# One read back ahead of the loads of v, and one output two products later, in a linear attention and SwiGLU kernel

## The chip, the core and the metric

The kernel runs on one core of a Trainium2 chip. Its engines work side by side: TensorE (PE in the profile: matrix products), VectorE (DVE), ScalarE (ACT), GpSimd (POOL) and SyncE (SP). Here SyncE only issues DMA transfers; GpSimd and ScalarE issue some too. Each engine takes its instructions in the order of its own queue, and a DMA whose buffer is not free yet holds up everything behind it in the queue that issues it. The metric is the device time of one execution in microseconds (us), lower is better.

## The reference

For 4 batches, 8 heads, 768 time steps and a head size of 48 a gated linear recurrence is computed. Its output goes through a SwiGLU block with 384 model dimensions and 1536 hidden ones.

```python
f = 1.0 / (1.0 + np.exp(-f_logit))
for t in range(S):
    state = f[:, :, t, :, None] * state + np.einsum('bhd,bhe->bhde', k[:, :, t], v[:, :, t])
    y[:, :, t] = np.einsum('bhd,bhde->bhe', q[:, :, t], state)
x = y.transpose(0, 2, 1, 3).reshape(B * S, H * D)
g = x @ w_gate
out = (g * (1.0 / (1.0 + np.exp(-g))) * (x @ w_val)) @ w_out
```

All tensors reach the kernel in float32, or as 64-bit words that it converts itself (the weights).

## The kernel before

The 768 steps are cut into 6 chunks of 128. A **unit** is one chunk of one batch, so there are 24; they are numbered u = 4 x chunk + batch from 0. Unit 5 is the second chunk's second unit, units 8 to 11 make up the third chunk. The attention of a unit replaces the recurrence by products within the chunk plus a carried state. Beside the attention of chunk c + 1 runs the SwiGLU block of chunk c: as plain products for the first chunk (gate and val at L940, down product o at L963), and with fewer products but more sums on VectorE from the second chunk on (L1156, L1259, L1322). The first part of the program, up to the block of the first chunk, works with the units 0 to 7; in it the weights are also converted.

`attention(u)` is a generator of 15 steps. What matters here, in order:

- Steps 1 to 4 turn the gates f and the decays (`gates`, `tails`) into the decayed k, `kT` (VectorE, L682 to L649).
- Step 5: `kT` is transposed in blocks (L723, into the room of the raw k) and written to DRAM as `turn` (L726, four transfers). Behind it the next unit's k is loaded into the same room (L498).
- Step 7: q is transposed (L741, into `tails`), and the next unit's q is loaded behind it. Step 8: q times the gates becomes `qT`. In the second chunk the step also loads the part of v that is needed beside A: `load_other_v` (L454, "A<-in_v_dram", two transfers). It writes into a corner of the score buffer `A`, of which there is one, so it waits until the previous unit's y products are done with it.
- Step 9: the scores `sc`. From the third chunk on this is where `load_other_v` is called, and then, for batches 0 to 2, `turn` is read back into `kt` (L784). There is one `kt`, read by the product dS. Step 10 masks the scores into `A`; in the second chunk, and for batch 3, it also holds the read back (L790).
- Step 12, the output: the products of y with the state (L837), the new state's product dS (L819, from `kt` and `v`), and the products of y with A (L848; L873 for the other units). Step 13 copies y out (L855) and sends it into `xT` (L862). From the third chunk on it also loads v of the unit after next (L506), into one of two `v` buffers, which this unit's products just read. Step 14 forms the state (L901).

The transfers of q, k, f, v, `turn` and `kt` are issued by GpSimd for units 5 to 7 (most of them) and by SyncE from unit 8 on.

The order of everything comes from due times written by hand. `EARLY` has one row of 15 times for each unit of the second chunk, one for each step. `times(c)` does the same for the later chunks: the output at time o, step 13 at o + 0.01, step 14 at o + 2.1. `in_turn_of_time` runs down the products of the SwiGLU block, counts 2.57 for each plain product, and calls every step whose time has come. The resulting order is then fixed for PE, VectorE, ScalarE and SyncE; for GpSimd it is fixed only in the later part, so in units 4 to 7 the scheduler may move GpSimd's instructions among each other.

Of the kernel before, what the change touches and what calls it, by code (L numbers as in the profile page):

```python
# [290 lines left out]
def short_path(ctx, tc, ident, least, judge, q, k, v, f_logit, moe_w_gate, moe_w_val, moe_w_out, out):  # L291
# [24 lines left out]
    SQUARES = 2  # L316
# [86 lines left out]
    def by_squares(u):  # L403
        return u >= SQUARES * B - 3
# [24 lines left out]
    def in_halves(u):  # L429

        b, c = units[u]
        return c > 0 and b < B - 1
# [10 lines left out]
    def other_v(A):  # L443

        return A.rearrange("p r a t -> p (r a t)")[:, 12 * CH:].rearrange("p (h e) -> p h e", e=W)

    def load_other_v(A, u):
        b, c = units[u]  # L450
        queue = nc.sync if c >= SQUARES or not by_squares(u) else nc.gpsimd
        for n in range(2):
            since = c * C + (1 - n) * CH
            queue.dma_start(out=other_v(A)[n * CH:(n + 1) * CH, :, 0:D],  # L454
                            in_=v[b, n * HP:(n + 1) * HP, since:since + CH, :].rearrange("h t d -> t h d"))
# [26 lines left out]
    def load(u, what="fkqv"):  # L482
        b, c = units[u]
        rows = slice(c * C, (c + 1) * C)
        inputs = dict(f=f_logit, k=k, q=q, v=v)
        for nm in "fqkv" if c >= SQUARES else "fvkq" if by_squares(u) else "fkqv":
            src = inputs[nm]
            if nm not in what:
                continue
            if nm == "v":  # L490
                dst = v_of(u)
            elif not by_squares(u):
                dst = raw[nm][u % NRAW]
            else:
                since = len(traced)
                for n in range(4):
                    at = Q * (1 - n % 2)
                    (nc.sync if c >= SQUARES else nc.gpsimd).dma_start(  # L498
                        out=rooms[nm][Q * n:Q * (n + 1), at:at + HP * RUN].rearrange("t (a e) -> t a e", a=HP),
                        in_=src[b, n // 2::2, rows, :].rearrange("a (t i) d -> t a (i d)", i=NI))  # L500
                if c < SQUARES:
                    by_pool.extend(ins for ins in traced[since:] if ins.engine == mybir.EngineType.Pool)
                    keep_order(by_pool[-5:])
                continue
            queue = nc.gpsimd if nm == "v" and c < SQUARES and (by_squares(u) or u in (1, 2)) else nc.sync
            queue.dma_start(out=dst[:, :, 0:D], in_=src[b, :, rows, :].rearrange("h t d -> t h d"))  # L506
# [118 lines left out]
    def attention(u):  # L625
        b, c = units[u]
# [13 lines left out]
        halves = in_halves(u)  # L640
# [75 lines left out]
        if turned:  # L716


            if u == SQUARES * B:
                A = att.tile([128, 2, HP, C], FP32, tag="A", name="A")  # L720
# [24 lines left out]
        if halves and c < SQUARES:  # L745
            A = att.tile([128, 2, HP, C], FP32, tag="A", name="A")
# [7 lines left out]
        if u != SQUARES * B and not (halves and c < SQUARES):  # L754
            A = att.tile([128, 2, HP, C], FP32, tag="A", name="A")
        flat = [A.rearrange("p r a t -> p (r a t)")[:, 6 * CH * par:6 * CH * par + 8 * CH] for par in range(2)]
        if halves and c >= SQUARES:
            load_other_v(A, u)
        sc = [score_bank(u) for _ in range(2)]
        for keys in range(2) if halves else ():  # L760
            for a in (0, 2, 1, 3):
# [20 lines left out]
        at_once = turned and c >= SQUARES and b < B - 1  # L782
        if at_once:
            turn_queue.dma_start(out=kt, in_=turn.rearrange("t i a r e -> i t (a r e)"))  # L784
        yield
        if not in_squares:
            nc.scalar.copy(least[:, u, :], whole.rearrange("p a t -> p (a t)"))
# [35 lines left out]
        if halves:  # L823
# [28 lines left out]
            def copy_y():  # L852
                yT = att.tile([128, 2, TB // 2], FP32, tag="x", name="yT")
                for par in range(2):
                    nc.scalar.copy(yT[:, par, :], y[par][:, 0:HP // 2 * C])  # L855
                for h in range(H):
                    a, par = h // 2, h % 2
                    f = h * D
                    while f < (h + 1) * D:
                        n = min((h + 1) * D, (f // 128 + 1) * 128) - f  # L860
                        r = W * (a % 2) + f - h * D
                        (nc.gpsimd if c >= SQUARES else nc.sync).dma_start(out=xT[c][f % 128:f % 128 + n, f // 128, b * C:(b + 1) * C],  # L862
                                                                           in_=yT[r:r + n, a // 2, par * C:(par + 1) * C])
                        f += n
# [26 lines left out]
            dS = new_state()  # L891
        if halves:
            copy_y()
        if c >= SQUARES and u + 2 < len(units):
            load(u + 2, "v")
        yield
        if c == 0:
            nc.scalar.copy(states[b], dS)
        elif c < NCH - 1:
# [133 lines left out]
    def score_bank(u):  # L1033
        b, c = units[u]
        kind = SCORES[c][b][1] if c >= SQUARES else "b"
        if kind == "b":
            return bank("sc")
        return {"o": banks_o, "A": banks_a}[kind].tile([128, 512], FP32, tag=kind, name="sc")
# [3 lines left out]
    FETCHES_AT = (-1.1, 0.6, 5.5, 5.9, 6, 9.2, 9.8, 19.9, 22.4, 25.8, 32.3, 32.7, 36.2, 40.8)  # L1042
    EARLY = (
# [4 lines left out]
    SUMS_AT = (64.3, 64.5, 72.98, 73.1, 74.46, 74.74, 75.3, 75.42, 75.98, 76.02, 76.18, 76.3, 76.66, 76.86,  # L1048
# [308 lines left out]
    mark = traced[-1]  # L1357
    keep_warm(5)
    first = [attention(b) for b in range(B)]
    done = [0] * B  # L1360

# [47 lines left out]
    for b, at in enumerate(EARLY):  # L1409
        run_of = attention(B + b)  # L1410
        waiting += [(t, lambda run_of=run_of: next(run_of)) for t in at]
# [23 lines left out]
    for c in range(2, NCH):  # L1435
        for b in range(B):
            run = attention(c * B + b)
            waiting += [((c - 2) * whole + t, lambda run=run: next(run)) for t in times(c)[b]]
# [21 lines left out]
def kernel(  # L1460
# [22 lines left out]
    def judge(bank):  # L1483
# [13 lines left out]
        yield  # L1497

    short_path(tc, ident, least, judge, *args)
    with tc.If(redo[0] > 0, label="redo"):  # L1500
        general_path(tc, *args)
# [32 lines left out]
```

## Time and profile before

| | |
|---|---|
| median of 3 runs | 596.11 us (595.91, 596.11, 599.32) |
| profiled execution | 598.69 us, of it 597.0 us span |
| mean granted TensorE clock | 0.99 |
| busy in the span | PE 579.3, DVE 471.9, ACT 306.5, POOL 119.3 us |
| moved by DMA | 64.48 MB, mean 108 GB/s |

The span is the time from the first to the last instruction of the profiled execution; the 1.7 us beside it lie around it. Busy times of different engines overlap. A row of the timeline gives start, length, engine and line of a group of instructions, the tile written and those read, and the count; in brackets stands the engine's idle time before the group and what ended it. PE works in fp32, in two passes, so a timeline counts 12 matmuls where the program has 6.

### The profile page before, as it was taken

How to read it: one execution, taken by the hardware profiler on the slowest of the kernel's cores; microseconds unless marked ns; L12 is line 12 of the kernel's file. 1: busy time of each engine (PE TensorE's matmuls, PEld its weight loads, DVE VectorE, ACT ScalarE, POOL GpSimd, SP SyncE). 2: the span in 40 equal slices, each digit the busy share in tenths (PEclk: the TensorE clock that was granted, in tenths of full speed). 3: DMA queues.
4: the chain of work that ended last, by engine and by line, in shares of the span. 5: the costliest groups of instructions: out<-in, count | busy, mean ns of one | idle time of the engine just before them, and what ended most of it. 6: DMA issues, size and time to landing. Idle time of an engine off the chain costs nothing.

```text
span 597.0 us, 12326 instructions
## 1 busy us (share of the span) xinstructions
PE 579.3 (97%) x4644; PEld 479.1 (80%) x4644; DVE 471.9 (79%) x828; ACT 306.5 (51%) x589; POOL 119.3 (20%) x257
## 2 busy tenths in 40 slices
PE   7899988999999989999999999999999999999996
PEld 5744434566888889888899988899988899988996
DVE  7978995899989966988995978995878982666641
ACT  3587785203777612476742376842276730356600
POOL 4140454311122150130330030311030320000000
PEclk9999997999999989999999999999999999999999
DMA  9999796224579565463444453444341100100001
GB/s 187 262 270 291 195 236 149 60 55 137 120 148 148 96 146 130 139 140 72 96 109 105 125 125 70 86 103 100 114 114 28 35 8 7 54 1 2 0 1 55
DMA packets 117825, 64.48 MB, mean 108 GB/s; under 512 B 75568, under 2 KB 108144, under 8 KB 117760
## 3 DMA queue, kind: packets, MB, share of 16 engines
q1 hardware_dynamic: 105360, 48.29, 33.7%
q0 software_dynamic: 11248, 13.78, 10.4%
q10 hardware_dynamic: 1152, 1.57, 0.7%
q8 instruction: 37, 0.61, 0.4%
q14 instruction: 28, 0.23, 0.1%
HBM read 49.64 MB, written 8.65 MB: 98 GB/s over the span
## 4 chain that ended last, share of the span: by engine, by line
PE 86%; DMA 5%; DVE 3%; ACT 3%; issue 1%; POOL 1%; SPq 0%; ACTq 0%; DVEq 0%; POOLq 0%
PE o L1259 19%; PE A L1156 17%; PE B L1156 14%; PE c L1156 5%; PE o L963 5%; PE o L1156 5%; PE gate L940 3%; PE o L1322 3%; DMA kt<-turn 3%; PE val L940 3%; PE y L873 2%; PE dS L819 2%; PE y L848 2%; PE y L837 2%; PE sc L764 1%
## 5 line engine op out<-in xcount | busy, mean ns | idle before, releaser
L862 POOL DMA_DIRECT2D xT<-yT x120 | 59.7, 506 | 62.1 <-ACT yT L855 59.4
L1259 PE MATMUL o<-w_out,h 128*128 128x192 f32 x360 | 62.0, 327 | 0.0
L1156 PE MATMUL A<-xs,w_both 128*128 128x256 f32 x240 | 61.8, 380 | 0.0
L1259 PEld LDWEIGHTS o<-w_out,h 128*128 128x128 f32 x360 | 58.8, 190 | 0.8 <-issue 0.4
L1161 ACT COPY aside<-A 128x512 f32<-128x512 f32 x60 | 35.1, 586 | 33.1 <-PE A L1156 33.1
L1057 DVE TENSOR_TENSOR c<-c,aside 128x512 f32<-128x512 f32 x60 | 41.2, 687 | 12.5 <-ACT aside L1161 10.8
L1156 PEld LDWEIGHTS A<-xs,w_both 128*128 128x128 f32 x240 | 45.2, 190 | 6.3
L1161 ACT COPY c<-A 128x512 f32<-128x512 f32 x40 | 23.3, 584 | 46.5 <-PE A L1156 46.5
L1108 DVE TENSOR_TENSOR h<-h,c 128x256 f32<-128x256 f32 x100 | 40.5, 414 | 5.9 <-ACT h L1172 5.6
L1060 DVE TENSOR_TENSOR c<-c,aside 128x512 f32<-128x512 f32 x60 | 41.0, 684 | 2.6 <-ACT aside L1161 2.5
L1259 PE MATMUL o<-ws,h 128*128 128x192 f32 x240 | 41.7, 328 | 0.0
L1172 ACT ACTIVATE h<-c 128x256 f32<-128x256 f32 x100 | 39.2, 416 | 4.8 <-DVE c L1057 3.5
L1156 PE MATMUL A<-xs,extra 128*128 128x256 f32 x160 | 41.3, 380 | 0.3 <-ACT c L1161 0.2
L1156 PE MATMUL B<-xs,w_both 128*128 128x256 f32 x160 | 41.3, 380 | 0.0
L1156 PE MATMUL B<-xT,extra 128*128 128x256 f32 x160 | 41.1, 379 | 0.0
L1156 PE MATMUL c<-xT,w_both 128*128 128x256 f32 x160 | 41.1, 379 | 0.0
L1259 PEld LDWEIGHTS o<-ws,h 128*128 128x128 f32 x240 | 39.3, 190 | 0.8 <-issue 0.5
L1161 ACT COPY aside<-B 128x512 f32<-128x512 f32 x60 | 35.1, 585 | 8.9 <-PE B L1156 7.0
L749 POOL MEMSET gates<- 128x4 f32 x24 | 3.3, 136 | 169.9 <-DVE qT L649 164.8
L1060 DVE TENSOR_TENSOR c<-o,c 128x512 f32<-128x512 f32 x40 | 27.4, 685 | 10.7 <-ACT h L1172 5.8
L1057 DVE TENSOR_TENSOR c<-c,o 128x384 f32<-128x384 f32 x15 | 8.2, 549 | 34.2 <-PE o L1259 34.2
L1156 PEld LDWEIGHTS A<-xs,extra 128*128 128x128 f32 x160 | 30.2, 190 | 5.1 <-ACT c L1161 1.1
(177 smaller groups left out, 1268.2 us busy)
## 6 DMA issues: line engine op xcount, KB each, us to landing
fsquares<-in_f_logit_dram SPq DMA_DIRECT2D x64, 96.0 KB, 4.5
qsquares<-in_q_dram SPq DMA_DIRECT2D x64, 96.0 KB, 2.3
ksquares<-in_k_dram SPq DMA_DIRECT2D x64, 96.0 KB, 2.5
w<-in_moe_w_gate_dram SPq DMA_DIRECT2D x6, 768.0 KB
w<-in_moe_w_val_dram SPq DMA_DIRECT2D x6, 768.0 KB, 7.4
w<-in_moe_w_out_dram SPq DMA_DIRECT2D x6, 768.0 KB, 9.8
v<-in_v_dram SPq DMA_DIRECT2D x19, 192.0 KB, 2.8
kt<-turn SPq DMA_DIRECT2D x12, 256.0 KB
```

The costliest lines, as they stand in the source:

```text
L819: nc.tensor.matmul(p[W * (h % 2):W * (h % 2) + W, (h // 2) * D:(h // 2 + 1) * D], lhsT=kt[:, h * W:(h + 1) * W], rhs=v_[:, h, 0:D], start= ...
L862: (nc.gpsimd if c >= SQUARES else nc.sync).dma_start(out=xT[c][f % 128:f % 128 + n, f // 128, b * C:(b + 1) * C], in_=yT[r:r + n, a // 2, ...
L940: nc.tensor.matmul(p, lhsT=w[:, j, i, :], rhs=xT[c][:, i, :], start=(i == 0), stop=(i == KT - 1))
L963: nc.tensor.matmul(p, lhsT=hidden_tile(h, n // 2)[:, n % 2 * 2 + b // 2, b % 2 * C:(b % 2 + 1) * C], rhs=w_out[:, j, :], start=(n == 0), s ...
L1057: nc.vector.tensor_tensor(dst, a, b, ALU.add)
L1060: nc.vector.tensor_tensor(dst, a, b, ALU.subtract)
L1108: lagging.append(lambda: f(*args))
L1156: nc.tensor.matmul(p[name][:, n, :], lhsT=weights_of[a][:, n, j, :], rhs=tokens[b], start=fresh and n == 0, stop=True, skip_group_check=True)
L1161: nc.scalar.copy(t, p[name])
L1172: nc.scalar.activation(dst, src[:, 0, :], AF.Silu)
L1259: nc.tensor.matmul(p[:, n, :], lhsT=lhsTs[j][:, n * C:(n + 1) * C], rhs=rhs[:, j, :], start=first and j == order[0] and n == 0, stop=j == ...
L1322: nc.tensor.matmul(p, lhsT=hidden_tile(h, j)[:, 2, n * C:(n + 1) * C], rhs=b22[:, j, :], start=j == order[0], stop=j == order[-1])
```

## The change

Three edits. In step 9, from the third chunk on, the read back of `kt` is issued ahead of `load_other_v`. The load of v for the unit after next moves from step 13 to step 14. And unit 5's step 12 gets the time 55.2 in place of 50.4.

```diff
-        if halves and c >= SQUARES:
-            load_other_v(A, u)
         sc = [score_bank(u) for _ in range(2)]
...
         if at_once:
             turn_queue.dma_start(out=kt, in_=turn.rearrange("t i a r e -> i t (a r e)"))
+        if halves and c >= SQUARES:
+            load_other_v(A, u)
         yield
...
         if halves:
             copy_y()
+        yield
         if c >= SQUARES and u + 2 < len(units):
             load(u + 2, "v")
-        yield
...
-        (26, 28.8, 29.3, 32.2, 32.3, 32.6, 35.3, 36.6, 37.4, 39.8, 42.5, 42.6, 50.4, 55.21, 56.4),
+        (26, 28.8, 29.3, 32.2, 32.3, 32.6, 35.3, 36.6, 37.4, 39.8, 42.5, 42.6, 55.2, 55.21, 56.4),
```

How this moves instructions: on TensorE, in the block of the first chunk, around unit 5's output (y and dS; gate and val are products of the SwiGLU block, o its first down product). First where the group begins, then where it ends:

```order
 L940 MATMUL gate<-xT,w_both 128x512 x6
 L940 MATMUL val<-xT,w_both 128x512 x6
+L940 MATMUL gate<-xT,w_both 128x512 x6
 L837 MATMUL y<-qT,decayed 32x128 x8
 L819 MATMUL dS<-v_125,kt 64x48 x8
...
 L848 MATMUL y<-A 48x64
 L848 MATMUL y<-A,v_125 64x64
-L940 MATMUL gate<-xT,w_both 128x512 x6
 L940 MATMUL val<-xT,w_both 128x512 x6
 L963 MATMUL o<-w_out,h 128x384 x4
```

One pair of gate products now runs before unit 5's output instead of behind it.

In GpSimd's queue, the stretch that follows unit 5's read back (the first row) and ends with unit 6's (the last row); `A` is unit 6's, `fraw`, `kraw` and `qraw` are loads for unit 7:

```order
 L790 DMA kt<-turn 128x1x512
 L498 DMA fraw<-in_f_logit_dram 32x4x192 x4
-L454 DMA A<-in_v_dram 64x4x48 x2
 L726 DMA turn<-kraw 512x1x32 x4
 L498 DMA kraw<-in_k_dram 32x4x192 x4
 L498 DMA qraw<-in_q_dram 32x4x192 x4
+L454 DMA A<-in_v_dram 64x4x48 x2
 L749 MEMSET gates_102 128x4
 L790 DMA kt<-turn 128x1x512
```

Unit 6's load into `A` has moved behind the `turn` writes and the loads of k and q, to just ahead of its read back. No edit names it; the scheduler put it there.

In SyncE's queue, around the read back of unit 10 (third chunk, third batch), before:

```order
L498 DMA qsquares<-in_q_dram 32x4x192 x4
L506 DMA v_125<-in_v_dram 128x8x48
L454 DMA A<-in_v_dram 64x4x48 x2
L784 DMA kt<-turn 128x1x512
L498 DMA fsquares<-in_f_logit_dram 32x4x192 x4
L726 DMA turn<-ksquares 512x1x32 x4
```

and with the change:

```order
L498 DMA qsquares<-in_q_dram 32x4x192 x4
L782 DMA kt<-turn 128x1x512
L454 DMA A<-in_v_dram 64x4x48 x2
L498 DMA fsquares<-in_f_logit_dram 32x4x192 x4
L506 DMA v_125<-in_v_dram 128x8x48
L726 DMA turn<-ksquares 512x1x32 x4
```

The read back comes first, then A, and `v` of unit 11 falls behind the load of f for unit 12.

## The prediction

> **What bounds the kernel now.** I read the page first: how busy each engine is, its clock, and the chain of work that ended last.
>
> ```profile
> PE 579.3 (97%) x4644; PEld 479.1 (80%) x4644; DVE 471.9 (79%) x828; ACT 306.5 (51%) x589; POOL 119.3 (20%) x257
> PEclk9999997999999989999999999999999999999999
> PE 86%; DMA 5%; DVE 3%; ACT 3%; issue 1%; POOL 1%; SPq 0%; ACTq 0%; DVEq 0%; POOLq 0%
> ```
>
> TensorE (PE) is busy 97% of the span and is 86% of the chain. So only two things are left to win: time in which PE stands still, and the slices in which its clock falls (7 and 8 in the second row). The list of who waited for whom, for PE alone, has one entry that counts after the start-up:
>
> ```profile
> PE dS L819 <- DMA kt<-turn: 6.3, 2, 4.3
> ```
>
> Two waits, 4.3 us and 2.0 us, both of the new-state product dS for `kt`, the decayed k read back from DRAM. PE's timeline says where they are (start, length, engine and line; in brackets the idle time before it and what ended it):
>
> ```profile
> 81.63 5.31 PE L940 MATMUL val<-xT,w_both 128*128 128x512 f32 x12
> 86.87 0.45 PE L837 MATMUL y<-qT,decayed 48*32 48x128 f32 x16
> 91.62 1.09 PE L819 MATMUL dS<-v,kt 128*64 128x48 f32 x16 [4.30 <-DMA kt<-turn]
> 94.56 6.79 PE L940 MATMUL gate<-xT,w_both 128*128 128x512 f32 x12
> 106.34 2.74 PE L963 MATMUL o<-w_out,h 128*128 128x384 f32 x8
> ...
> 115.20 0.45 PE L837 MATMUL y<-qT,decayed 48*32 48x128 f32 x16
> 115.58 0.67 PE L819 MATMUL dS<-v,kt 128*64 128x48 f32 x16
> 117.23 8.01 PE L963 MATMUL o<-w_out,h 128*128 128x384 f32 x24
> ...
> 214.03 0.45 PE L837 MATMUL y<-qT,decayed 48*32 48x128 f32 x16
> 216.47 0.83 PE L819 MATMUL dS<-v,kt 128*64 128x48 f32 x16 [1.99 <-DMA kt<-turn]
> ```
>
> The first wait is in unit 5 (second chunk, second batch), the one whose output moves. The group at 115.20 is the next unit, 6, which did not wait. The second wait is in unit 10 (third chunk, third batch). Both stalls are followed by slow matmuls: dS takes 1.09 us at 91.62 and 0.67 at 115.58. The table of busy time by stretches of 3.41 us shows why (length, PE busy, granted clock, DMA share, GB/s):
>
> ```profile
> 8.60:12.02 3.42, 2.13 (x25) 1.00 1.06 208
> 87.11:90.52 3.41, 0.21 (x16) 1.00 1.03 254
> 90.52:93.94 3.42, 2.32 (x40) 0.50 0.92 199
> 93.94:97.35 3.41, 3.41 (x28) 0.50 0.60 152
> 213.41:216.82 3.41, 1.42 (x33) 1.00 0.97 176
> 216.82:220.23 3.41, 3.41 (x76) 0.50 0.34 65
> ```
>
> After each stall the clock is 0.50, for two stretches the first time and one the second. A stretch with 1.42 us of work was followed by half clock, one with 2.13 us was not.
>
> **What the edits remove.** Unit 5 first. From 86.87 to the first output product at 106.34 PE takes 19.47 us. In the new order it does the gate products (12 matmuls, 86.87 - 81.63 = 5.24 us at full clock), then the y group with its dS (117.23 - 115.20 = 2.03 us as in unit 6), then the val products (5.24): 12.51 us. The difference is **6.96 us**. Taken the other way, 4.30 of wait plus half of the 5.73 us from 91.62 to 97.35 is 7.17, so the two agree. What hides the rest of the transfer is the gate work: `kt` lands just before 91.62, and dS would now start at 86.87 + 5.24 + 0.38 = 92.49, 0.9 us behind it.
>
> Unit 10 waits because its read back stands behind two loads in SyncE's queue (the last row is unit 9's dS on PE):
>
> ```profile
> 195.96 4.52 SPq L498 DMA_DIRECT2D qsquares<-in_q_dram  x4
> 207.47 0.38 SPq L506 DMA_DIRECT2D v<-in_v_dram  x1
> 207.95 1.87 SPq L454 DMA_DIRECT2D A<-in_v_dram  x2
> 209.88 0.56 SPq L784 DMA_DIRECT2D kt<-turn  x1
> ...
> 205.67 0.67 PE L819 MATMUL dS<-v,kt 128*64 128x48 f32 x16
> ```
>
> SyncE is done with its q loads at 200.5 and waits for unit 9's y products, whose `v` and `A` the two loads reuse. The read back needs only the `kt` buffer, free once unit 9's dS is done (205.67 + 0.67 = 206.3). It could then be issued at 206.4 instead of 209.88. With the 6.6 us from issue to 216.47 that it took, it lands at 213.0, ahead of dS at 214.48. That removes 1.99 us and one stretch at half clock (3.41 / 2 = 1.70), **3.69 us**. I cost the moved loads at nothing: A would go out from about 207.0 to 208.9, a little earlier than now, and its products come behind dS; `v` is for the unit after this one and has that whole unit's work as cover. Without that cover PE would wait for a load instead, by as much as it is late. The `fsquares` load behind them waits for VectorE's transpose of unit 11 in both orders, so SyncE passes no delay on.
>
> **What the edits add.** The output's later place also changes an order nobody edited: in GpSimd's queue unit 6's load of `A` falls from ahead of the `turn` writes to directly ahead of unit 6's read back. That read back was the next one to be late anyway:
>
> ```profile
> 79.21 0.72 POOL L790 DMA_DIRECT2D kt<-turn  x1
> 94.98 1.24 POOL L454 DMA_DIRECT2D A<-in_v_dram  x2 [5.87 <-PE y L848]
> 96.21 2.58 POOL L726 DMA_DIRECT2D turn<-kraw  x4
> 100.58 1.09 POOL L498 DMA_DIRECT2D kraw<-in_k_dram  x2 [0.44 <-DMA turn<-kraw]
> 105.64 2.18 POOL L498 DMA_DIRECT2D qraw<-in_q_dram  x4 [3.97 <-DVE tails L741]
> 109.70 0.73 POOL L790 DMA_DIRECT2D kt<-turn  x1 [1.58 <-issue]
> ...
> DMA to landing us min/median/max: 5.1/5.1/5.1
> ```
>
> The last row is the landing of the read back at 109.70: 114.8, only 0.8 us ahead of dS at 115.58. PE would now be there 6.96 earlier, at 108.62. How far does the GpSimd chain move? It hangs on VectorE:
>
> ```profile
> 94.78 0.35 DVE L901 TENSOR_TENSOR state<-decayed,dS 128x192 f32<-128x192 f32 x1
> 95.05 0.70 DVE L723 STREAM_TRANSPOSE kraw<-kT 128x512 f32<-128x512 f32 x1
> 104.03 0.69 DVE L1108 TENSOR_TENSOR h<-h,val 128x512 f32<-128x512 f32 x1 [7.09 <-PE val L940]
> 104.64 0.71 DVE L741 STREAM_TRANSPOSE tails<-qraw 128x512 f32<-128x512 f32 x1
> ```
>
> The transpose at 95.05 waited for nothing, so it does not come earlier: `turn` goes out at 96.0, and the k loads, which wait for it to land, end near 101.5. The q loads were held by the transpose at 104.64, behind a product that waited 7.09 us for val. That wait goes, so they follow at once: 101.5 to 103.7. Then A (1.24, to 104.9), then the read back at 105.0, or at 106.6 if the unexplained 1.58 us recurs. Plus 5.1, it lands at 110.1 to 111.7: a **new wait of 1.5 to 3.1 us** where there was none. Bounds from rows farther off: nothing (a wait can't be less), if the queue runs freer than I think; 8.7 us, if the transfer takes the 12.3 us of unit 5's (79.21 to about 91.5). Unit 6's own row is the nearest, so I take 2.3 us.
>
> A gap of 2.3 us leaves 1.1 us of work in a stretch if it falls inside one, which the 1.42 row says costs a stretch at half clock (1.70); divided between two stretches it may cost nothing, and like the first stall it could cost two (2.9). I take 1.3. Together the new wait is **3.6 us**.
>
> [...]
>
> Nothing else is late next as far as VectorE goes. It has little air from here to the next block:
>
> ```profile
> 101.00:104.00 3.00, 3.00 (x8) 1.33 (x7) 0.00 (x0) 2.98 (x4) 0.67 (x2) 1.00 0.46 120
> 115.00:130.00 15.00, 15.00 (x175) 9.51 (x178) 14.55 (x25) 1.76 (x5) 3.35 (x6) 1.00 0.24 49
> 130.00:145.00 15.00, 15.00 (x88) 9.37 (x79) 15.00 (x30) 3.55 (x6) 1.92 (x7) 1.00 0.34 92
> ```
>
> (The third busy time is DVE's: 14.55 and 15.00 of 15 us.) But the 7.09 us it lost waiting for val come back to it, so it moves forward by as much as PE.
>
> **Sum.** 6.96 + 3.69 - 3.6 = 7.05 us. The profiled execution took 598.69, so 591.6. The median of the runs shown is 596.11, 2.58 lower. I can't tell whether those runs lose that less elsewhere (then 589.1) or in just these stalls, whose clock part is a matter of where the gap falls (then less can be won, and 591.6 holds: the highest and the lowest run are 3.41 us apart, one clock stretch). I take the middle, **590.4 us**.
>
> **Rivals.**
> - *Unit 6's read back is in time.* 10.65 us gained: 588.0, or 585.5 from the median. For it: the DMA share is low there (0.46 at 101). Against it: it was in time by only 0.8 us, and A now stands ahead.
> [...]
> - *VectorE gives the first gain back*: if it cannot follow, PE waits for its sums where the next block begins, and only unit 10's 3.69 is left: 595.0 or 592.4. Against it is the 7.09 row.
> - *The queue edit doesn't do what it says*: the read back stays behind something else and unit 10 still waits. 6.96 - 3.6 = 3.4 gained: 595.3 or 592.7. Against it: from 200.5 on SyncE only waits.
> - *Slower*: unit 6's read back meets traffic as unit 5's did (12.3 us to land). From 105.0 it lands at 117.3: a wait of 8.7 and 2.9 of clock, 11.6 against 10.65, so 599.6 or 597.1; with the 1.58 us also, 601.2. It decides from a landing at about 116.4. Against it: unit 5's ran while the DMA share was 1.03 and 0.92, and from 93.94 on it is 0.60 and less.
>
> **How the numbers follow.** Forecast with a new wait and its clock 0.52; read back in time 0.16; new wait without clock 0.12; VectorE 0.08; queue edit without effect 0.07; slower 0.05. A measurement can tell about 1%, so faster means under 590.15: all of the second case, most of the third, under half of the first, 0.45. Slower by over 1% (above 602.1) is the tail of the last, 0.02; the rest, 0.53, is within 1%. The range of 586 to 595 takes in both ends of the forecast (585.5 + 1.5 = 587.0 from the median with the short wait and no clock, 588.0 + 3.1 + 2.9 = 594.0 from the profile with the long one) and most of the cases beside it; some 0.12 is left out.
>
> **What would show it.** Right: no bracket before dS of units 5 and 10; everything on PE behind unit 10 some 7 us earlier; in unit 6 a bracket of 1.5 to 3.1 us before dS near 108.6, released by `kt<-turn`, and a stretch at 0.50 behind it. In GpSimd's timeline A ends directly ahead of the read back, near 105. Wrong: if unit 6 has no bracket, the landing was faster than 5.1 or the chain began earlier than 96; if unit 5 keeps one, its transfer took longer than 12.3; if a wait of PE for VectorE shows between 100 and 145, VectorE did not follow.

## The result, and the profile after

| | before | changed kernel |
|---|---|---|
| median, on the chip of the first comparison | 596.97 us (595.91 to 599.32) | 590.38 us (589.97 to 591.68) |
| median, on a second chip | 598.19 us (595.61 to 599.94) | 590.84 us (590.26 to 592.67) |
| profiled execution | 598.69 us, span 597.0 | 591.68 us, span 590.0 |
| PE busy in the span | 579.3 us | 577.0 us |

The ratio to the time before is 0.9888, with a 95% interval of 0.9852 to 0.9925; on the second chip 0.9887 (0.9863 to 0.9911). Forecast were 590.4 us, and from profiled to profiled execution 7.05 us less; it was 598.69 - 591.68 = 7.01. Two executions of the kernel before, of 605.14 and 3411.76 us on the chip of the first four experiments, count as slow and are in no ratio.

The page has the same engines at the same work. What differs is PE's clock, one fall fewer to be seen in the slices:

```profile
PE 577.0 (98%) x4644; PEld 477.0 (81%) x4644; DVE 471.8 (80%) x828; ACT 306.0 (52%) x589; POOL 118.5 (20%) x257
PEclk9999999899999999999999999999999999999999
PE 85%; DVE 5%; ACT 3%; DMA 3%; issue 2%; POOL 1%; DVEq 0%; ACTq 0%; POOLq 0%
```

The list of PE's waits has one wait of dS where there were two, of 1.8 us in all against 6.3:

```profile
PE dS L819 <- DMA kt<-turn: 1.8, 1, 1.8
```

PE's timeline places it (start, length, engine and line; the bracket holds the idle time before):

```profile
86.52 5.31 PE L940 MATMUL gate<-xT,w_both 128*128 128x512 f32 x12
91.76 0.45 PE L837 MATMUL y<-qT,decayed 48*32 48x128 f32 x16
92.14 0.67 PE L819 MATMUL dS<-v,kt 128*64 128x48 f32 x16
...
99.05 2.74 PE L963 MATMUL o<-w_out,h 128*128 128x384 f32 x8
...
107.91 0.45 PE L837 MATMUL y<-qT,decayed 48*32 48x128 f32 x16
110.16 0.67 PE L819 MATMUL dS<-v,kt 128*64 128x48 f32 x16 [1.81 <-DMA kt<-turn]
...
140.47 1.03 PE L1156 MATMUL A<-xs,w_both 128*128 128x256 f32 x4
...
210.62 0.67 PE L819 MATMUL dS<-v,kt 128*64 128x48 f32 x16
```

Unit 5's dS at 92.14 and unit 10's at 210.62 have no bracket. Unit 6's at 110.16 has one now. The row at 140.47 opens the next block; before it stood here:

```profile
144.26 1.03 PE L1156 MATMUL A<-xs,w_both 128*128 128x256 f32 x4
```

So the first down product (99.05) starts 7.29 us earlier than the 106.34 of before, the next block only 3.79 us. The 3.50 us between are the new wait, 1.81, and the half clock behind it (length, PE's busy time first, then the other engines; granted clock, DMA share, GB/s):

```profile
107.59:111.00 3.41, 1.60 (x42) 0.99 (x44) 3.27 (x6) 0.00 (x0) 0.82 (x2) 1.00 0.13 49
111.00:114.42 3.42, 3.42 (x43) 2.56 (x36) 2.10 (x5) 1.05 (x3) 1.75 (x3) 0.50 0.52 83
```

A stretch of 3.42 us at 0.50 costs 1.71 by my estimate, and 1.81 + 1.71 = 3.52; on PE, from unit 6's dS to the row at 140.47 it took 30.31 us, 1.63 more than before (28.68, from 115.58 to 144.26). The rest of the gain, 7.01 - 3.79 = 3.22 us, comes behind 140.47, from unit 10. (On PE itself it is 3.44: its last products start at 580.51 in place of 587.74. The other 0.2 us are lost behind PE's end.)

GpSimd's timeline shows what unit 6's read back stood behind, the last row its time from issue to landing:

```profile
95.79 2.56 POOL L726 DMA_DIRECT2D turn<-kraw  x4 [6.95 <-DVE least L734]
100.00 1.12 POOL L498 DMA_DIRECT2D kraw<-in_k_dram  x2 [0.24 <-DMA turn<-kraw]
101.11 2.18 POOL L498 DMA_DIRECT2D qraw<-in_q_dram  x4
103.27 1.24 POOL L454 DMA_DIRECT2D A<-in_v_dram  x2
104.50 0.12 POOL L749 MEMSET gates<- 128x4 f32 x1
105.17 0.73 POOL L790 DMA_DIRECT2D kt<-turn  x1 [0.55 <-issue]
...
DMA to landing us min/median/max: 4.9/4.9/4.9
```

105.17 + 4.9 = 110.07, and dS starts at 110.16. In SyncE's queue unit 10's read back now goes out at 202.59, right behind unit 9's dS; what the loads lost by it cost nothing that PE shows:

```profile
202.59 0.57 SPq L782 DMA_DIRECT2D kt<-turn  x1
203.71 2.22 SPq L454 DMA_DIRECT2D A<-in_v_dram  x2
206.04 2.20 SPq L498 DMA_DIRECT2D fsquares<-in_f_logit_dram  x4
208.30 0.65 SPq L506 DMA_DIRECT2D v<-in_v_dram  x1
```

### The profile page after: what moved, and what is told of

Same layout as the page of the kernel before. It is cut to its first block, busy times and chain, and to the rows that moved or that the text cites. A ratio compares the mean times of both kernels' runs of the same rounds, so it can differ in the third digit from the quotient of the medians.

```text
span 590.0 us, 12330 instructions
## 1 busy us (share of the span) xinstructions
PE 577.0 (98%) x4644; PEld 477.0 (81%) x4644; DVE 471.8 (80%) x828; ACT 306.0 (52%) x589; POOL 118.5 (20%) x257
## 4 chain that ended last, share of the span: by engine, by line
PE 85%; DVE 5%; ACT 3%; DMA 3%; issue 2%; POOL 1%; DVEq 0%; ACTq 0%; POOLq 0%
PE o L1259 20%; PE A L1156 17%; PE B L1156 14%; PE c L1156 6%; PE o L1156 5%; PE o L963 4%; PE o L1322 3%; PE gate L940 2%; PE y L873 2%; DMA fraw<-in_f_logit_dram 2%; PE dS L819 2%; PE val L940 2%; PE y L837 2%; PE y L848 2%; PE sc L762 1%
```

## The experiments

The first four ran on one chip (before there: 598.71 us), the next three on another (598.19), the last two on a third (597.93). All times are medians; ratios are to before on the same chip. Where the difference of the medians and the ratio say different amounts, the ratio has the interval.

| kernel | us | ratio, 95% interval |
|---|---|---|
| unit 5's output alone | 594.40 | 0.9959 (0.9927 to 0.9991) |
| read back alone | 594.85 | 0.9960 (0.9929 to 0.9992) |
| v's load alone | 597.85 | 0.9996 (0.9968 to 1.0024) |
| changed, A first | 589.87 | 0.9875 (0.9817 to 0.9932) |
| changed, again | 590.84 | 0.9887 (0.9863 to 0.9911) |
| changed, unit 6 later | 590.56 | 0.9874 (0.9852 to 0.9896) |
| changed, read back ahead of q | 588.27 | 0.9838 (0.9813 to 0.9862) |
| the same, again | 588.73 | 0.9843 (0.9816 to 0.9870) |
| changed, both | 588.41 | 0.9834 (0.9809 to 0.9860) |

**Unit 5's output alone.** The kernel before with one number changed:

```diff
-        (26, 28.8, 29.3, 32.2, 32.3, 32.6, 35.3, 36.6, 37.4, 39.8, 42.5, 42.6, 50.4, 55.21, 56.4),
+        (26, 28.8, 29.3, 32.2, 32.3, 32.6, 35.3, 36.6, 37.4, 39.8, 42.5, 42.6, 55.2, 55.21, 56.4),
```

> The kernel before with unit 5's output two products later, and SyncE's queue as before. Theory: the two edits act in two places and add up. Unit 5's wait of 4.3 us and the half clock behind it go (7.0 us), unit 6 gets a wait of about 1.8 us for its read back, with or without 1.7 us of half clock, and unit 10 keeps its wait of 2.0 us and the stretch at half clock. Span 3.5 to 5.2 us under the kernel before. Rival: the queue edit brings the whole gain, because the later output only trades unit 5's wait for unit 6's; then the span is within 1 us of the kernel before.

By the medians 4.3 us less, by the ratio 2.5 (0.5 to 4.4). Unit 5 has no bracket any more; unit 6 got one, and unit 10 kept its own:

```profile
111.25 0.67 PE L819 MATMUL dS<-v,kt 128*64 128x48 f32 x16 [2.83 <-DVE gates L737]
212.49 0.67 PE L819 MATMUL dS<-v,kt 128*64 128x48 f32 x16 [2.33 <-DMA kt<-turn]
```

So this edit alone brings both the first gain and the new wait. (The bracket at 111.25 names a VectorE scan that dS does not read. The read back that it does read was issued at 105.41 and took 5.7 us, to 111.1.) Neither gap was followed by half clock, though both are longer than the 1.81 us that was:

```profile
106.05:109.46 3.41, 2.37 (x23) 1.02 (x21) 3.21 (x7) 0.00 (x0) 0.09 (x1) 1.00 0.21 63
109.46:112.87 3.41, 1.62 (x56) 1.56 (x56) 2.57 (x6) 0.00 (x0) 2.58 (x4) 1.00 0.29 53
112.87:116.29 3.42, 3.42 (x19) 2.07 (x12) 1.57 (x4) 1.06 (x3) 0.68 (x1) 1.00 0.32 58
```

The stretches are those of the clock's records: before and in the changed kernel every change between 1.00 and 0.50 lies a whole number of times 3.41 us behind the first record (25, 27, 62, 63 and 173 times before, 31, 32 and 171 in the changed kernel). Where they lie against the program differs from one execution to the next: here one begins at 106.05, in the profiled changed kernel at 107.59. The gap of 2.83 us fell across two of them; each kept 1.62 us of work or more.

**The read back alone.** The kernel before with the first edit of the change only.

```diff
-        if halves and c >= SQUARES:
-            load_other_v(A, u)
...
             turn_queue.dma_start(out=kt, in_=turn.rearrange("t i a r e -> i t (a r e)"))
+        if halves and c >= SQUARES:
+            load_other_v(A, u)
```

> The kernel before with only the read back moved ahead of the load into A; the load of v stays at step 13 and so still stands ahead of the read back in SyncE's queue, waiting for unit 9's y products. Theory: the read back of unit 10 goes out near 207.9 instead of 209.9 and lands near 214.5, so that its wait falls from 2.0 to 0 to 0.5 us and the stretch at half clock goes: 3 to 3.7 us under the kernel before. Units 5 and 6 as in the kernel before (4.3 us and none). Rival: unit 10's wait does not come from the queue's order; then it stays at 2.0 us and the time is the same.

3.9 us less by the medians, 2.4 (0.5 to 4.2) by the ratio. SyncE still issues v first here, then the read back; dS of unit 10 does not wait:

```profile
205.94 0.38 SPq L506 DMA_DIRECT2D v<-in_v_dram  x1
206.37 0.57 SPq L782 DMA_DIRECT2D kt<-turn  x1
207.04 1.74 SPq L454 DMA_DIRECT2D A<-in_v_dram  x2
...
212.88 0.67 PE L819 MATMUL dS<-v,kt 128*64 128x48 f32 x16
```

Passing A's load is enough. Unit 5 still waits, for 4.06 us (the bracket there names a VectorE instruction; `kt`, issued at 78.95, took 12.0 us to land, to 90.95, and dS starts at 91.13). But it has one stretch of half clock where the profile before had two, which is no effect of this edit:

```profile
85.40:88.81 3.41, 1.68 (x20) 0.41 (x18) 3.38 (x6) 3.40 (x5) 2.17 (x4) 1.00 1.03 239
88.81:92.22 3.41, 1.09 (x32) 1.06 (x36) 3.34 (x6) 2.65 (x3) 0.02 (x1) 1.00 1.04 273
92.22:95.64 3.42, 3.42 (x35) 2.07 (x28) 3.35 (x8) 0.00 (x0) 1.23 (x2) 0.50 0.69 163
```

**v's load alone.** The kernel before with `load(u + 2, "v")` behind the `yield`, in step 14.

> The kernel before with only the load of v moved to step 14. The read back of unit 10 still stands behind the load into A, which waits for unit 9's y products. Theory: only the 0.5 us of the load of v are saved ahead of the read back, so unit 10 still waits about 1.5 us, with or without the stretch at half clock: 0.5 to 2.2 us under the kernel before. Rival: the load of v is what holds the read back; then unit 10's wait is gone and the time 3.7 us lower.

No difference that the interval can tell from nothing, where 0.5 to 2.2 us less were expected, and unit 10 waits nearly as long as before (1.99):

```profile
216.95 0.67 PE L819 MATMUL dS<-v,kt 128*64 128x48 f32 x16 [1.80 <-DMA kt<-turn]
```

Unit 5, which this edit does not touch, waited 5.67 us in this profile against 4.30 before. So waits of this kind differ by over 1 us from one execution to the next.

By the ratios the two effective edits alone save 0.41% and 0.40%, the whole change 1.1%. The intervals are too wide to say whether the two add up.

**A first.** The changed kernel, with unit 6's load into A called in step 5 and held ahead of the `turn` writes. My prediction had named A's new place as a part of the new wait.

```diff
+            if u == SQUARES * B - 2:
+                since = len(traced)
+                A = att.tile([128, 2, HP, C], FP32, tag="A", name="A")
+                load_other_v(A, u)
             nc.vector.transpose(beside.rearrange("p i (a e) -> p a i e", e=Q), kT.rearrange("p a (i e) -> p a i e", e=Q))
...
+            if u == SQUARES * B - 2:
+                keep_order([ins for ins in traced[since:] if ins.engine == mybir.EngineType.Pool])
...
-        if halves and c < SQUARES:
+        if halves and c < SQUARES and u != SQUARES * B - 2:
```

> The changed kernel, with unit 6's load into A issued in step 5 and kept ahead of the turn writes in GpSimd's queue. Theory: the load of 1.24 us ahead of the read back is part of unit 6's new wait. With it gone from there the read back goes out near 103.9 to 104.5 instead of 105.17 and unit 6 waits 0.5 to 1.2 us instead of 1.8, with no half clock behind it: span 1 to 3 us under the profiled run of the changed kernel. Rival: the chain of k and q loads sets the read back and the load into A only fills a gap; then the wait stays at 1.8 us.

That part of my theory was not borne out. GpSimd and dS, with A out of the way:

```profile
100.53 1.09 POOL L498 DMA_DIRECT2D kraw<-in_k_dram  x2 [0.62 <-DMA turn<-kraw]
101.61 2.18 POOL L498 DMA_DIRECT2D qraw<-in_q_dram  x4
...
104.70 0.72 POOL L796 DMA_DIRECT2D kt<-turn  x1 [0.80 <-issue]
...
110.19 0.67 PE L825 MATMUL dS<-v,kt 128*64 128x48 f32 x16 [1.83 <-DMA kt<-turn]
```

The read back goes out 0.47 us earlier (104.70 against 105.17), not 1.24, for with A ahead of the `turn` writes the last k loads come later (100.53 against 100.00). It takes 5.4 us to land instead of 4.9, and so lands no earlier; the wait is 1.83 us as before. Behind the q loads the landing takes 4.9 to 5.7 us over the profiles, which is more scatter than the 0.47. The span, 588.1 us, does lie 1.9 us under the 590.0 of the profiled changed kernel, as I had expected, but for another reason: the clock stayed. From dS to the next down product it took 1.65 us (110.19 to 111.84), in the profiled changed kernel, at 0.50, 2.35 (110.16 to 112.51).

**The changed kernel again.**

> The changed kernel once more, on one chip with the next two. Theory: unit 6 waits 1.8 us or somewhat more for its read back and units 5 and 10 don't wait; the stretch at half clock behind unit 6 comes in some executions and not in others. Span 588 to 590.5 us.

The wait was 2.44 us this time:

```profile
110.78 0.67 PE L819 MATMUL dS<-v,kt 128*64 128x48 f32 x16 [2.44 <-DMA kt<-turn]
```

The clock stayed at 1.00, for the gap lay across two stretches, with 1.78 and 2.62 us of work:

```profile
106.57:109.99 3.42, 1.78 (x21) 0.70 (x19) 3.21 (x7) 0.00 (x0) 0.00 (x0) 1.00 0.25 76
109.99:113.40 3.41, 2.62 (x59) 2.23 (x60) 3.28 (x7) 0.80 (x3) 2.65 (x4) 1.00 0.35 53
```

**Unit 6 later.** The same remedy as for unit 5: unit 6's output one down product later.

```diff
-        (45.4, 48.4, 50.3, 51, 51.1, 58.6, 58.8, 59.2, 62.8, 63.9, 64.4, 65.5, 68.2, 68.21, 70),
+        (45.4, 48.4, 50.3, 51, 51.1, 58.6, 58.8, 59.2, 62.8, 63.9, 64.4, 65.5, 70.9, 70.91, 71),
```

> The changed kernel, with unit 6's output one down product later (2.6 us of work more ahead of it). Theory: that covers the wait of 1.8 us, so no dS after the start-up waits, no stretch at half clock is left, and the span is 1.8 us (without the clock's part) to 3.5 us (with it) under the changed kernel: near 586.5. Rival: as the later output of unit 5 did, this one only hands the wait on to the next unit, 7, whose read back then is late by as much; the time stays within 0.5 us of the changed kernel.

About 586.5 us of span were expected; it is 588.8, and the median is that of the changed kernel beside it (590.56 and 590.84). The wait of dS went and another took its place at once, as long as the old one within the scatter:

```profile
109.89 2.85 PE L963 MATMUL o<-w_out,h 128*128 128x384 f32 x8 [1.83 <-DVE w_out L559]
```

The down product pulled forward needs a part of `w_out` that VectorE has not converted yet. PE was 7 us ahead of the old schedule, and two engines were late for it, not one: GpSimd with the read back and VectorE with the weights. The rival had the time right, but named the next unit's read back as what would be late. The stretch that holds this gap had 1.59 us of work, and the next one ran at full clock:

```profile
106.47:109.89 3.42, 1.59 (x5) 0.57 (x4) 3.21 (x7) 0.00 (x0) 0.00 (x0) 1.00 0.24 75
109.89:113.30 3.41, 3.41 (x32) 1.87 (x34) 1.76 (x3) 0.00 (x0) 2.53 (x4) 1.00 0.27 41
```

**The read back ahead of q.** The changed kernel, with unit 6's read back called in step 7, ahead of the loads of q, and held there in GpSimd's queue. The orders on PE, VectorE, ScalarE and SyncE stay.

```diff
+            if u == SQUARES * B - 2:
+                kt = att.tile([128, HP * C], FP32, tag="kt", name="kt")
+                since = len(traced)
+                turn_queue.dma_start(out=kt, in_=turn.rearrange("t i a r e -> i t (a r e)"))
             qp = tail[:, 0:HP * C]
             nc.vector.transpose(parted(qp), split_squares("q"))
             load_after(u, "qv" if c < SQUARES else "q")
+            if u == SQUARES * B - 2:
+                mine = [ins for ins in traced[since:] if ins.engine == mybir.EngineType.Pool]
+                keep_order(mine[:1] + mine[-4:])
...
-            if turned:
+            if turned and u != SQUARES * B - 2:
                 turn_queue.dma_start(out=kt, in_=turn.rearrange("t i a r e -> i t (a r e)"))
...
```

> The changed kernel, with unit 6's read back ahead of the loads of q in GpSimd's queue (it was behind them and behind the load into A); PE's order is that of the changed kernel. Since taking the load into A away from there did not shorten the wait, the theory is now that the loads of q hold the read back, by their place in the queue and by their own transfers: it would go out near 101.6 in place of 105.2, land near 107, and dS at 108.3 would not wait. Span 1.8 to 3.5 us under the changed kernel. Rival: the read back is slow for its own sake or late for another reason; then a wait of over 1 us is left.

588.27 us, 2.6 less than the changed kernel beside it on the same chip, and the slowest of these five executions (589.11) is faster than the fastest of those six (590.26). In GpSimd's and PE's timeline, with the landing of the read back between them:

```profile
101.36 0.69 POOL L743 DMA_DIRECT2D kt<-turn  x1
102.05 2.19 POOL L498 DMA_DIRECT2D qraw<-in_q_dram  x4
104.86 1.24 POOL L454 DMA_DIRECT2D A<-in_v_dram  x2 [0.62 <-issue]
...
DMA to landing us min/median/max: 7.1/7.1/7.1
108.64 0.67 PE L826 MATMUL dS<-v,kt 128*64 128x48 f32 x16
110.20 0.31 PE L855 MATMUL y<-A 64*48 64x128 f32 x1 [0.31 <-DMA A<-in_v_dram]
```

The read back goes out 3.8 us earlier. With the q loads right behind it, it takes 7.1 us instead of 4.9, lands at 108.46, and dS does not wait. Now A is late next, by 0.31 us.

**The same again, and both moves together.** The last kernel has the edits of "A first" and of "read back ahead of q".

> The kernel with only the read back ahead of the q loads, again, as the one to compare with: no wait of dS, 0.3 us of wait for A in unit 6, a time of 588.0 to 589.1, and 0.984 of the time before.

> The changed kernel with both moves in GpSimd's queue: unit 6's load into A ahead of the turn writes (in step 5), and unit 6's read back ahead of the q loads (in step 7). With the read back first but A last, dS did not wait, the first product y<-A waited 0.31 us for A, and from dS to the next down product it took 2.37 us instead of 1.66. My theory: A had no part in the wait of dS but is late next once dS does not wait, so with A first too that stretch is back at 1.66, nothing in unit 6 waits, and the time is 0.7 us lower than with the read back alone (588.27 there), near 587.6. The rival: A's transfers ahead of turn delay the turn writes, and so the k loads and the read back, by the 1.24 us that they take to issue; the read back stood 7 us early by its issue, so that costs dS nothing, but the q loads behind it move too, and VectorE's work for unit 7 is late instead: same time or up to 1 us more, 588.3 to 589.3.

With both, nothing in unit 6 waits, and from dS to the next down product it takes 1.65 us:

```profile
108.30 0.67 PE L832 MATMUL dS<-v,kt 128*64 128x48 f32 x16
109.95 8.01 PE L976 MATMUL o<-w_out,h 128*128 128x384 f32 x24
```

The medians differ by 0.32 us (588.41 and 588.73), which the intervals can't tell apart; the 0.7 I expected was not reached, since in its second profile the read back alone took 1.90 us there, not the 2.37 of its first. Nor has that profile a bracket for A. So A's place, which I had blamed, is worth a few tenths at most. Both versions are faster than the kernel before and the changed kernel.

## Why the prediction was right, and where it was not

- **Unit 5, 6.96 us.** The first down product starts 7.29 us earlier. 0.35 of that is there already where the moved products begin (86.52 against 86.87), so the term is 6.94. The gate products cover the rest of the transfer as forecast: it left at 78.39, took 12.8 us, and landed at 91.2, 0.9 us before dS at 92.14 (forecast 92.49).
- **Unit 10, 3.69 us.** 3.22 us came behind 140.47 (3.44 on PE itself), and with the read back alone 3.9 by the medians, 2.4 (0.5 to 4.2) by the ratio. The read back went out 0.05 us after unit 9's dS ended (202.59 against 201.87 + 0.67), as worked out. Moving v's load contributed nothing by itself.
- **The new wait, 1.5 to 3.1 us, taken 2.3.** It came: 1.81 and 2.44 us in the two profiles of the changed kernel, released by `kt<-turn`. The chain on GpSimd ran as worked out (q loads to 103.29, forecast 103.7; read back at 105.17, forecast 105.0 or 106.6; landing at 110.07, forecast 110.1 to 111.7).
- **A as a part of that wait was not borne out.** I read "directly ahead" in the queue as a price of 1.24 us. With A gone from there the read back left only 0.47 us earlier and dS waited 1.83 us all the same; with the read back ahead of both the q loads and A, the wait was gone. "A first" and "both" differ in the order of the read back and the q loads alone, with A out of the way in each: in its profile the first waits 1.83 us, the second not at all. So the place behind the 2.18 us of the q loads decided, and those I had treated as given. A few tenths for A are not excluded.
- **The clock term, 1.3 us, was mis-sized.** One stretch at half clock lowers an execution's mean clock by about 1.7 / 590 = 0.003, by my estimate; the profiled execution with one had 0.996, the second profile without one 0.999. Of the ten executions of the changed kernel three had a mean clock of 0.996 or 0.997, seven 0.998 or more. So the typical cost is nothing, and 3 in 10 of 1.7 is 0.5 on average. The case "new wait without clock" describes most executions, the forecast the profiled one.
- **The base.** I took the middle between 591.6 and 589.1, since the three runs shown had a median 2.58 below the profiled one and I could not tell where they lose less. The mean clocks of the kernel before beside the experiments tell it, for 45 executions on three chips. At a clock of 0.988 to 0.991 there were 27, of 597.7 to 600.6 us; at 0.993 or 0.994 eight, of 596.8 to 598.5; at 0.995 or 0.996 eight, of 595.0 to 597.4; at 0.999 two, of 593.2 and 593.3. So most of the difference between runs goes with the clock, which is the reading for which I had 591.6, and the profiled execution (0.990) is the usual case. 591.6 less the 0.8 by which the clock term was too high is 590.8, near the median on the second chip (590.84). On the chip of the first comparison the base was 596.97, 0.43 under the 597.40 that the middle stands for, and the gain by the medians 6.59, 0.46 under 7.05. These two errors ran against each other, and the hit to 0.02 us is luck.
- **VectorE followed**, but with less air than I thought. One conversion of weights, which stood at 120.29 without a wait before, now waits 3.19 us for PE (the first row is before, the second the changed kernel):

```profile
120.29 0.96 DVE L559 CUSTOM_DVE_ANT_0 w_out<-top,up 128x1536 uint16<-128x1536 uint16 x1
...
116.32 0.96 DVE L559 CUSTOM_DVE_ANT_0 w_out<-top,up 128x1536 uint16<-128x1536 uint16 x1 [3.19 <-PE o L963]
```

By its bracket the conversion writes a buffer that PE's down products must have left. It delayed nobody in the changed kernel; in the kernel with unit 6 later another of these conversions was what PE waited for.
- **What stays open.** Unit 5's read back took 12.3 us to land before and 12.8 in the changed kernel, unit 6's 5.1 and 4.9. Over these transfers the DMA share was 1.04 and 1.05 for unit 5, 0.17 and 0.21 for unit 6, which fits contention, but that was not tried: no run took that traffic away. The load of v was moved alone, and in the whole change; the change without it was not run, so what its move is worth beside the other two edits is not shown.

## What to carry to other kernels

When a stall goes, the engine arrives earlier behind it (here 7.29 us at the first down product): for each thing it waits for there, write down when that lands and by how much it was in time. Here unit 6's margin of 0.8 us against a move of 7 said at once that it would be late, and the cure was not to move the consumer again (another engine was late too) but to issue the transfer ahead of loads that nobody needs so soon. Which of the things queued ahead of a late transfer holds it up is to be tried one by one; the one that moved last need not be it.

## What the runs showed that I had not expected

**The clock fell with the work in one stretch of 3.41 us, not with the length of the gap.** Gaps of 1.81 us (the changed kernel) and 1.99 us (before) were followed by 3.41 us at 0.50; gaps of 2.83 and 2.33 (unit 5's output alone), 2.44 (changed, again), 1.83 (A first) and 1.80 us (v's load alone) were not. PE's work in the stretch sorts them: with 0.21 and 1.42 (before), 1.09 (read back alone) and 1.60 us (the changed kernel) of 3.41 the next stretch ran at 0.50; with 1.62 and 1.71 (unit 5's output alone), 1.68 (read back alone) and 1.78 (changed, again) at 1.00. One stretch of 1.59 (unit 6 later) was followed by 1.00 against this order. The ends of matmuls are modelled in the profile, so a hundredth means little; from these stretches I estimate a border near 1.6 us for this kernel. Behind a stretch at 0.50 with 2.32 us of work (before, from 90.52) came another at 0.50, behind one with 3.42 (the changed kernel, from 111.00) the full clock. So the wait of 1.81 us in the changed kernel had a stretch at half clock behind it, an estimated 1.7 us, and the wait of 2.44 us in its second profile had none. A part of the scatter between runs of one kernel goes with the clock: the kernel before took 597.7 to 600.6 us at a mean of 0.988 to 0.991, and 593.2 and 593.3 at 0.999.

**A transfer that leaves earlier can take longer.** The same read back landed in 4.9 to 5.7 us behind the q loads, and in 7.1 where it went out just ahead of them. Of the 3.8 us that it left earlier than in the changed kernel 2.2 were given back, and it was in time by 0.2. With both moves it left at 101.58 and dS ran at 108.30 without a wait, so it landed within 6.7 us.
